# w_val decoded one tile per block, and two small matrix groups per block formed in the layer-1 banks

## The chip, the cores and the metric

One core of a Trainium2 chip runs the whole program. The metric is the device time of one execution in microseconds (us), as the median of three runs. TensorE (PE in the profile, its weight loads PEld) multiplies and writes to PSUM, of which this kernel uses all eight banks; VectorE (DVE) and ScalarE (ACT) read PSUM and work on SBUF; GpSimd (POOL) works on SBUF alone; SyncE (SP) issues nearly all transfers.

## What is computed

Eight batches (blocks b = 0 to 7) of 512 tokens go through an attention against 32 state rows per head, a normalised feed-forward layer with ReLU, and a gated layer, all in float32. The reference, cut:

```python
a = softmax(scale * x @ state.T);  xread = a @ state            # 512 tokens a block
a2 = softmax(scale * state @ x.T); sread = a2 @ x               # 32 tokens a block
x = concat(xread, sread)                                        # (8, 544, 512)
xn = (x - mu) / sqrt(var + 1e-6) * g_ln
x = x + maximum(xn @ w_ch1, 0) @ w_ch2
gate = sigmoid(causal_conv5(x, conv_w)); val = x @ w_val
out = (gate * val) @ w_out
```

(The concatenation stands for the kernel's two parts: 8 blocks of 512 tokens and, as a ninth block, the 8 x 32 tokens of sread.) The weights arrive as 64-bit floats and are decoded on the chip.

## The kernel before

**Precision.** Every large product is made of three fp32r matmuls (`mm3`, L76 to L79: high times low, low times high, high times high), so the lines L77, L78 and L79 carry nearly all of TensorE's time. An operand is split into a high and a low half by `split_sb` (L72: an ACT copy at L73, a subtraction at L74 on DVE or POOL).

**Loop.** `segment` (L590) goes through a block in 16 steps f, one for each 128 rows of the hidden layer. TensorE's order is written out by hand (the calls stand under `manual_schedule` for PE); the other engines' orders are made by a scheduler that goes by `at_prio` values and by its own estimate of when inputs are ready. In a step, TensorE computes layer 1 of step f (six matmuls of 512 columns into one of the two `ps_mm` banks, called h), then layer 2 of step f-1 (`second`, twelve matmuls into the four `ps_acc` banks). Layer 1's result goes through ACT (`hid`, L646) and DVE (L648) and is layer 2's operand in the next step.

**Matrix groups.** Layer 1 does not multiply the normalised tokens with `w_ch1`: for every quarter q of the hidden layer, `m_steps(b, q)` (L131) first multiplies the block's states into `w_ch1`. A group is eight small matmuls (L137, 64 rows by 32 columns of the array each, 512 columns of data, float32), four into the bank mp[0] and four into mp[1]; DVE then reads each bank once (L143, into `mb`) and ACT (L73) and POOL (L74, DVE in blocks 0 and 1) split it into `m`. There are 32 groups, four for each block, made at f = 1, 5 and 9 for the block's next quarter and at f = 13 for the next block's first. The banks come from the pool `ps_at` of two, which the scores (L188), the transposes (L261) and the column sums (L298) use too. Before, a group stands ahead of layer 1 of its step.

**Background.** At the end of each step `next(bg)` advances a generator. In blocks 2 to 7 it is `background(b)` (L910): first `x1_var` (L339), the variance of the block, whose last part (`rstd_of`, L301) comes after four empty steps; then `attention_steps(b + 1)` (L405) for the next block: scores (L188, same shape as the matrix groups, into two `ps_at` banks), the two softmaxes on DVE and ACT (L192 to L223, L242 to L253), the transposes (L261, full array) and `sread` (L275, small matmuls); then the next loads. After the last step of block 2 comes `prep_weights` for `w_val` (L902): four tiles, each loaded (L470, 512 KB) and decoded by `decode_split` (ACT L485 and L487, DVE L493, L495, L496, L500, then the split: ACT L73, DVE L74) into a tile called `raw`. At a block's last step whatever is left of the generator is run out.

**Block boundary.** Layer 2 of step 15 is drained by DVE (L675, four reads of the `ps_acc` banks, each followed by an addition L678); in step 1 of the next block `x1_group` (L313) writes the four `ps_acc` banks (L318), and ACT (L325) and DVE (L323) read two each.

## Time and profile before

| what | value |
|---|---|
| median of three runs | 910.47 us (910.41 to 911.41) |
| profiled execution: its own time | 910.09 us |
| its span, first to last instruction | 908.0 us |
| PE busy | 887.1 us (98% of the span) |
| DVE, ACT, POOL busy | 595.7, 381.9, 216.3 us |
| mean granted TensorE clock | 0.996 |

The profiled execution lies 0.38 us under the median. Sums below are made against its time. The granted clock is full (1.00) in every block. A full-size matmul (128 x 512) is shown 0.39 us long, but they are pipelined: starts lie 0.23 us apart. So gaps on TensorE are read from the starts, and "PE busy" says little; where TensorE stood still is seen in the lengths of equal stretches and in the idle times of the timeline.

### The profile page before, as it was taken

How to read it: one execution, taken by the hardware profiler on the slowest of the kernel's cores; microseconds unless marked ns; L12 is line 12 of the kernel's file. 1: busy time of each engine (PE TensorE's matmuls, PEld its weight loads, DVE VectorE, ACT ScalarE, POOL GpSimd, SP SyncE). 2: the span in 40 equal slices, each digit the busy share in tenths (PEclk: the TensorE clock that was granted, in tenths of full speed). 3: DMA queues.
4: the chain of work that ended last, by engine and by line, in shares of the span. 5: the costliest groups of instructions: out<-in, count | busy, mean ns of one | idle time of the engine just before them, and what ended most of it. 6: DMA issues, size and time to landing. Idle time of an engine off the chain costs nothing.

```text
span 908.0 us, 12667 instructions
## 1 busy us (share of the span) xinstructions
PE 887.1 (98%) x4987; PEld 668.5 (74%) x4988; DVE 595.7 (66%) x1030; ACT 381.9 (42%) x699; POOL 216.3 (24%) x172
## 2 busy tenths in 40 slices
PE   8988989999999999999999999999999999999998
PEld 3345657777777677777777777777789988888886
DVE  6998998486366663445437246342469799988870
ACT  4755654144253433324234233332327555455532
POOL 0001020012322522522342152253200023432100
PEclk9999999999999999999999999999999999999999
DMA  9932220022013111110111110110121212222122
GB/s 363 375 116 76 73 74 1 1 96 99 8 43 96 73 50 51 49 49 2 51 50 47 50 47 1 27 47 1 47 93 48 93 50 90 93 94 93 54 86 70
DMA packets 26667, 66.44 MB, mean 73 GB/s; under 512 B 10864, under 2 KB 13040, under 8 KB 22512
## 3 DMA queue, kind: packets, MB, share of 16 engines
q1 hardware_dynamic: 25984, 65.24, 20.1%
q8 instruction: 39, 0.64, 0.3%
q10 hardware_dynamic: 624, 0.40, 0.2%
q14 instruction: 20, 0.16, 0.1%
HBM read 47.80 MB, written 17.83 MB: 72 GB/s over the span
## 4 chain that ended last, share of the span: by engine, by line
PE 81%; DVE 12%; DMA 3%; ACT 1%; issue 1%; SPq 0%; DVEq 0%; ACTq 0%
PE acc L77 15%; PE acc L79 15%; PE acc L78 15%; PE mm L77 9%; PE mm L78 8%; PE mm L79 8%; PE at L137 3%; PE at L77 2%; PE at L79 2%; PE at L78 2%; DVE w L496 1%; DVE w L500 1%; DMA x1d<-t 1%; DVE hid L648 1%; DVE raw L496 1%
## 5 line engine op out<-in xcount | busy, mean ns | idle before, releaser
L77 PE MATMUL acc<-hid,w 128*128 128x512 f32 (+1 forms) x560 | 213.0, 380 | 2.2 <-DVE x L323 1.3
L78 PE MATMUL acc<-hid,w 128*128 128x512 f32 (+1 forms) x560 | 211.7, 378 | 0.0
L79 PE MATMUL acc<-hid,w 128*128 128x512 f32 (+1 forms) x560 | 211.6, 378 | 0.0
L648 DVE SCALAR_TENSOR_TENSOR hid<-mm,hid 128x512 fp32r<-128x512 f32 (+1 forms) x140 | 92.0, 657 | 141.4 <-ACT hid L646 141.2
L646 ACT ACTIVATE hid<-mm 128x512 fp32r<-128x512 f32 (+2 forms) x144 | 82.4, 572 | 216.6 <-PE mm L79 212.9
L77 PEld LDWEIGHTS acc<-hid,w 128*128 128x128 f32 x560 | 105.4, 188 | 25.3 <-DVE hid L648 2.2
L77 PE MATMUL mm<-ahl,m 128*128 128x512 f32 (+1 forms) x312 | 120.3, 385 | 0.0
L79 PEld LDWEIGHTS acc<-hid,w 128*128 128x128 f32 x560 | 105.4, 188 | 19.9
L78 PEld LDWEIGHTS acc<-hid,w 128*128 128x128 f32 x560 | 105.5, 188 | 19.5
L78 PE MATMUL mm<-ahl,m 128*128 128x512 f32 (+1 forms) x312 | 115.5, 370 | 0.3 <-DVE m L74 0.3
L79 PE MATMUL mm<-ahl,m 128*128 128x512 f32 (+1 forms) x312 | 115.5, 370 | 0.0
L724 DVE SCALAR_TENSOR_TENSOR ahl<-big,cw,ahl 128x508 f32<-128x508 f32 (+3 forms) x128 | 101.8, 845 | 0.2
L74 POOL TENSOR_TENSOR m<-mb,m 128x512 fp32r<-128x512 f32 x48 | 65.4, 1377 | 142.3 <-ACT m L73 142.3
L77 PEld LDWEIGHTS mm<-ahl,m 128*128 128x128 f32 x312 | 59.1, 189 | 40.7 <-issue 28.3
L73 ACT ACTIVATE m<-mb 128x512 fp32r<-128x512 f32 x62 | 39.0, 629 | 81.6 <-DVE mb L143 81.2
L79 PEld LDWEIGHTS mm<-ahl,m 128*128 128x128 f32 x312 | 59.0, 189 | 10.1
L78 PEld LDWEIGHTS mm<-ahl,m 128*128 128x128 f32 x312 | 59.2, 190 | 9.2 <-DVE m L74 1.0
L710 POOL TENSOR_TENSOR w<-big,w 128x512 fp32r<-128x512 f32 x24 | 38.6, 1636 | 93.1 <-ACT w L708 93.1
L143 DVE SCALAR_TENSOR_TENSOR mb<-cs,sbn,at 128x512 f32<-128x512 f32 x62 | 43.5, 743 | 21.9 <-PE at L137 20.9
L79 PE MATMUL acc<-w,raw 128*128 128x512 f32 (+1 forms) x144 | 54.4, 378 | 0.0
L78 PE MATMUL acc<-w,raw 128*128 128x512 f32 (+1 forms) x144 | 54.4, 378 | 0.0
L77 PE MATMUL acc<-w,raw 128*128 128x512 f32 (+1 forms) x144 | 54.4, 378 | 0.0
(178 smaller groups left out, 1332.1 us busy)
## 6 DMA issues: line engine op xcount, KB each, us to landing
w<-in_w SPq DMA_DIRECT2D x20, 512.0 KB, 7.1
big<-in_xT SPq DMA_DIRECT2D x8, 1024.0 KB, 4.9
big<-in_xk SPq DMA_DIRECT2D x8, 1024.0 KB, 5.6
x2d<-x SPq DMA_DIRECT2D x8, 1024.0 KB, 3.9
big<-x2d SPq DMA_DIRECT2D x8, 1024.0 KB, 4.8
out<-hid SPq DMA_DIRECT2D x16, 512.0 KB, 2.8
raw<-in_w SPq DMA_DIRECT2D x12, 512.0 KB, 6.7
raw<-in_wval SPq DMA_DIRECT2D x4, 512.0 KB, 3.6
```

Source lines behind the costliest of these rows:

```text
L73: nc.scalar.activation(hi, src, AF.Copy)
L74: eng.tensor_tensor(lo, src, hi.bitcast(F32), op=ALU.subtract)
L77: nc.tensor.matmul(acc, lhsT=wh, rhs=xl, start=first, stop=False)
L78: nc.tensor.matmul(acc, lhsT=wl, rhs=xh, start=False, stop=False)
L79: nc.tensor.matmul(acc, lhsT=wh, rhs=xh, start=False, stop=last)
L137: nc.tensor.matmul(mp[u][32 * p:32 * p + 32, :], lhsT=stg[r, p, :], rhs=w1s[4 * q + p][r], start=True, stop=True)
L143: a = nc.vector.scalar_tensor_tensor(mb, cs[:, q], sbn[:, u], mp[u], op0=ALU.mult, op1=ALU.add)
L496: a = nc.vector.tensor_scalar(h[:, :, 0, 1], h[:, :, 1, 1], 0x8000, 0x4000, op0=ALU.bitwise_and, op1=ALU.bitwise_or)
L646: marks["act"] = nc.scalar.activation(hid[:, 0], h, AF.Relu)
L648: marks["dve"] = nc.vector.scalar_tensor_tensor(hid[:, 1], h, 0.0, hid[:, 0].bitcast(F32), op0=ALU.max, op1=ALU.subtract)
L710: nc.gpsimd.tensor_tensor(lo, src, hi.bitcast(F32), op=ALU.subtract)
L724: t = nc.vector.scalar_tensor_tensor(g[:, j:], x[:, :n - j], cw_sb[:, k, PAD - j:TAPS - j], g[:, j:], op0=ALU.mult, op1=ALU.add)
```

## The change

1. `m_steps` takes a flag `mm`: with it, the two banks come from `ps_mm`, the pool of layer 1's h. In every group the order of the eight matmuls becomes four for mp[0], then four for mp[1], where they alternated.
2. In blocks 2 to 6, the groups of f = 5 and f = 9 use that flag and are formed after layer 2 of the step, directly ahead of the background's work, with another priority for their readers (`base - 500` where `base - 1500` stood).
3. `x1_var` has one empty step less and `attention_steps` one more behind the first softmax: variance, scores, softmaxes and transposes come one step earlier, `sread` and the loads stay. In block 7 an empty step keeps the sread block where it was.
4. `w_val` is no longer decoded at the end of block 2: in step 3 of blocks 3, 4, 5 and 6 one tile is loaded and decoded.

```diff
-    def m_steps(b, q):
+    def m_steps(b, q, mm=False):
         stg, _, sbn, _ = coef[b]
-        mp = [at_ps([P, S]) for _ in range(2)]
-        for p in range(KT):
-            for u in range(2):
+        mp = [ps(ps_mm, "mm", [P, S]) if mm else at_ps([P, S]) for _ in range(2)]
+        for u in range(2):
+            for p in range(KT):
                 r = slice(64 * u, 64 * u + 64)
...
         hl = halves_of(sqs[0], S)
-        yield
         yield
         yield
         yield
...
         softmax1_out(b)
         mean_terms(b)
         yield
+        yield
         sread(b)
...
+            later = 1 < b < B - 1 and f in (5, 9)
-            if b < B and unit is not None and f % QF == (2 if unit == (1, 0) else 1) and not fresh:
+            if b < B and unit is not None and f % QF == (2 if unit == (1, 0) else 1) and not fresh and not later:
                 at_prio(base - 1500)
                 m_steps(*unit)
...
             pend[0] = second
+            if later:
+                at_prio(base - 500)
+                m_steps(*unit, mm=True)
             at_prio(base + 500)
             next(bg, None)
...
+    val_weights = []
+
     def background(b):
         yield
-        yield from x1_var(b)
+        if b == 3:
+            val_weights.append(prep_weights(wval, wv, ["raw"] * KT))
+        for i, _ in enumerate(x1_var(b)):
+            if i == 2 and val_weights:
+                next(val_weights[0], None)
+            yield
         if b + 1 < B:
             yield from attention_steps(b + 1)
         else:
+            yield
             yield from sread_block_steps()
-        if b == 2:
-            yield from prep_weights(wval, wv, ["raw"] * KT)
```

How the built programs' instructions stand, at three places. In the rows, an operation's output is left of the arrow and its operands right, with the buffers' numbers; lines of the changed kernel behind L600 are one to four higher than those of the kernel before.

Place A, TensorE in block 4, before, at step 5: the end of layer 2 of step 3, the group for q = 2 (in `at` banks), layer 1 of step 5.

```order
L79 MATMUL acc3_589_3275<-hid_599_3327,w2_3_92_443 128x512
L137 MATMUL at_602_3364<-w1_4_156_772,stg_509_2811 32x512
L137 MATMUL at_603_3365<-w1_4_156_772,stg_509_2811 32x512
L137 MATMUL at_602_3364<-w1_4_156_772,stg_509_2811 32x512
L137 MATMUL at_603_3365<-w1_4_156_772,stg_509_2811 32x512
L137 MATMUL at_602_3364<-w1_5_167_830,stg_509_2811 32x512
L137 MATMUL at_603_3365<-w1_5_167_830,stg_509_2811 32x512
L137 MATMUL at_602_3364<-w1_5_167_830,stg_509_2811 32x512
L137 MATMUL at_603_3365<-w1_5_167_830,stg_509_2811 32x512
L77 MATMUL mm_607_3383<-ahl_543_3010,m_575_3224 128x512
```

The same group now, behind layer 2 of step 4, and directly behind it the scores of the next block (six more L188 rows follow, then layer 1 of step 6, whose bank is that of `mm_601`).

```order
L79 MATMUL acc3_580_3239<-hid_595_3325,w2_4_112_516 128x512
L137 MATMUL mm_601_3370<-w1_4_156_772,stg_498_2753 32x512 x2
L137 MATMUL mm_601_3370<-w1_5_167_830,stg_498_2753 32x512 x2
L137 MATMUL mm_602_3371<-w1_4_156_772,stg_498_2753 32x512 x2
L137 MATMUL mm_602_3371<-w1_5_167_830,stg_498_2753 32x512 x2
L188 MATMUL at_609_3397<-big_551_3092,st_raw_549_3088 32x512
L188 MATMUL at_610_3398<-big_551_3092,st_raw_549_3088 32x512
```

The group moved behind eighteen full matmuls and stands in a row with the scores, which in the kernel before come a step later, alone. At step 9 the group likewise stands directly ahead of the eight transposes L261.

Place B, DVE at the end of block 2 and the beginning of block 3, before: the third and fourth tile of `w_val` (`c_455`, `c_458`) between the reads of the `ps_acc` banks (L675), the matrix group (L143) and the copies L323.

```order
L495 TENSOR_SCALAR c_455_2515<-c_455_2515 128x512
L496 TENSOR_SCALAR raw_454_2513<-raw_454_2513 128x512
L675 TENSOR_TENSOR t2_465_2573<-acc1_365_1971,t2_463_2562 128x512
L648 SCALAR_TENSOR_TENSOR hid_462_2559<-mm_461_2552,hid_462_2559 128x512
L675 TENSOR_TENSOR t2_466_2579<-acc2_366_1975,t2_463_2562 128x512
L500 ISA c_455_2515<-raw_454_2513,c_455_2515 128x1024
L675 TENSOR_TENSOR t2_467_2585<-acc3_367_1979,t2_463_2562 128x512
L143 SCALAR_TENSOR_TENSOR mb_471_2601<-cs_7_84,sbn_393_2141,at_468_2590 128x512
L143 SCALAR_TENSOR_TENSOR mb_472_2605<-cs_7_84,sbn_393_2141,at_469_2591 128x512
L74 TENSOR_TENSOR raw_456_2522<-c_455_2515,raw_456_2522 128x512
L323 COPY x1_473_2609<-acc1_475_2611 128x512
L493 TENSOR_SCALAR c_458_2527<-c_458_2527 128x512
```

The same place now (L676 and L649 are L675 and L648 of before).

```order
L649 SCALAR_TENSOR_TENSOR hid_450_2511<-mm_449_2504,hid_450_2511 128x512
L676 TENSOR_TENSOR t2_453_2525<-acc1_365_1971,t2_451_2514 128x512
L676 TENSOR_TENSOR t2_454_2531<-acc2_366_1975,t2_451_2514 128x512
L676 TENSOR_TENSOR t2_455_2537<-acc3_367_1979,t2_451_2514 128x512
L143 SCALAR_TENSOR_TENSOR mb_459_2553<-cs_7_84,sbn_391_2119,at_456_2542 128x512
L143 SCALAR_TENSOR_TENSOR mb_460_2557<-cs_7_84,sbn_391_2119,at_457_2543 128x512
L323 COPY x1_461_2561<-acc1_463_2563 128x512
L323 COPY x1_461_2561<-acc3_465_2565 128x512
```

The decode rows are gone from the boundary; what is left there is the sequence that the boundary of blocks 3 and 4 has in the kernel before.

Place C, DVE in block 4, steps 3 to 6, before: layer 1's results of steps 3 and 4, the group for q = 2, the result of step 5.

```order
L648 SCALAR_TENSOR_TENSOR hid_599_3327<-mm_598_3320,hid_599_3327 128x512
L648 SCALAR_TENSOR_TENSOR hid_601_3349<-mm_600_3342,hid_601_3349 128x512
L143 SCALAR_TENSOR_TENSOR mb_605_3375<-cs_7_84,sbn_510_2813,at_602_3364 128x512
L143 SCALAR_TENSOR_TENSOR mb_606_3379<-cs_7_84,sbn_510_2813,at_603_3365 128x512
L648 SCALAR_TENSOR_TENSOR hid_608_3390<-mm_607_3383,hid_608_3390 128x512
```

Now: the five operations of one `w_val` tile between the results of steps 3 and 4, the variance's two (L304, L306), and the group's two reads behind the result of step 5, ahead of the scores' transposes L192.

```order
L649 SCALAR_TENSOR_TENSOR hid_590_3291<-mm_589_3284,hid_590_3291 128x512
L493 TENSOR_SCALAR c_592_3308<-c_592_3308 128x512
L496 TENSOR_SCALAR raw_591_3306<-raw_591_3306 128x512
L495 TENSOR_SCALAR c_592_3308<-c_592_3308 128x512
L500 ISA c_592_3308<-raw_591_3306,c_592_3308 128x1024
L74 TENSOR_TENSOR raw_593_3315<-c_592_3308,raw_593_3315 128x512
L649 SCALAR_TENSOR_TENSOR hid_595_3325<-mm_594_3318,hid_595_3325 128x512
L304 STREAM_TRANSPOSE t2_597_3343<-at_596_3340 128x512
L306 TENSOR_SCALAR rstd_598_3345<-t2_597_3343 128x16
L649 SCALAR_TENSOR_TENSOR hid_600_3355<-mm_599_3348,hid_600_3355 128x512
L143 SCALAR_TENSOR_TENSOR mb_604_3381<-cs_7_84,sbn_499_2755,mm_601_3370 128x512
L143 SCALAR_TENSOR_TENSOR mb_605_3385<-cs_7_84,sbn_499_2755,mm_602_3371 128x512
```

What moved: the tile's five operations came in, and the two L143 went from ahead of the result of step 5 to behind it. On DVE at step 9 the group's L143 likewise follow the result of step 9, ahead of which stand one L217 and two L223 of the first softmax.

## Rows read from the trace of the kernel before

**Rows 1.** The page's chain of work that ended last, shares by engine.

```profile
PE 81%; DVE 12%; DMA 3%; ACT 1%; issue 1%; SPq 0%; DVEq 0%; ACTq 0%
```

**Rows 2.** Blocks 2, 3, 4: length; PE, PEld, DVE, ACT, POOL busy; granted clock; DMA.

```profile
217.25:294.12 76.87, 76.75 (x468) 57.66 (x461) 45.65 (x80) 29.83 (x54) 23.30 (x18) 1.00 0.17 58
294.12:374.96 80.84, 78.86 (x468) 57.68 (x461) 43.99 (x76) 27.59 (x50) 28.24 (x22) 1.00 0.14 49
374.96:450.63 75.67, 75.67 (x469) 57.47 (x461) 36.71 (x66) 25.21 (x46) 26.22 (x22) 1.00 0.13 45
```

**Rows 3.** PE timeline, beginning of block 3: start, length, operation, idle before and releaser.

```profile
294.12 2.63 PE L318 MATMUL acc<-aT,sn_raw 32*64 32x512 f32 x12
297.99 0.50 PE L77 MATMUL mm<-ahl,m 128*128 128x512 f32 x1
...
301.79 0.39 PE L79 MATMUL acc<-hid,w 128*128 128x512 f32 x1
303.49 0.50 PE L77 MATMUL acc<-hid,w 128*128 128x512 f32 x1 [1.31 <-DVE x L323]
```

**Rows 4.** DVE timeline of the same place.

```profile
292.05 1.86 DVE L496 TENSOR_SCALAR raw<-raw 128x512 uint16<-128x512 uint16 x1
...
298.17 1.10 DVE L74 TENSOR_TENSOR raw<-c,raw 128x512 fp32r<-128x512 f32 x1
...
300.38 0.47 DVE L493 TENSOR_SCALAR c<-c 128x512 f32<-128x512 f32 x1 [0.51 <-ACT c L485]
300.88 1.40 DVE L495 TENSOR_SCALAR c<-c 128x512 uint32<-128x512 uint32 x1
...
302.73 0.71 DVE L323 COPY x<-acc 128x512 f32<-128x512 f32 x1
```

**Rows 5.** One group on the tiles `raw`, 270 to 306.5 us: least, median, greatest ns.

```profile
L500 DVE CUSTOM_DVE_ANT_0 c<-raw,c x4: 671/693/808, 282.1 to 303.4; 128x1024 uint16<-128x1024 uint16 x4
```

**Rows 6.** PE timeline in block 4 and at its beginning.

```profile
374.96 1.21 PE L318 MATMUL acc<-aT,sn_raw 32*64 32x512 f32 x16
376.10 0.50 PE L77 MATMUL mm<-ahl,m 128*128 128x512 f32 x1
...
392.81 0.39 PE L79 MATMUL acc<-hid,w 128*128 128x512 f32 x1
393.13 1.09 PE L137 MATMUL at<-w,stg 64*32 64x512 f32 x16
394.15 0.50 PE L77 MATMUL mm<-ahl,m 128*128 128x512 f32 x1
394.49 0.39 PE L78 MATMUL mm<-ahl,m 128*128 128x512 f32 x1
...
421.79 1.04 PE L261 MATMUL at<-ident,t 128*128 128x128 f32 x8
422.58 0.48 PE L77 MATMUL mm<-ahl,m 128*128 128x512 f32 x1
...
430.93 1.10 PE L275 MATMUL mm<-big,t 128*32 128x64 f32 x64
431.96 1.09 PE L137 MATMUL at<-w,stg 64*32 64x512 f32 x16
432.98 0.50 PE L77 MATMUL mm<-ahl,m 128*128 128x512 f32 x1
```

**Rows 7.** DVE timeline in block 4.

```profile
391.15 0.69 DVE L648 SCALAR_TENSOR_TENSOR hid<-mm,hid 128x512 fp32r<-128x512 f32 x1 [3.33 <-ACT hid L646]
394.39 1.41 DVE L143 SCALAR_TENSOR_TENSOR mb<-cs,sbn,at 128x512 f32<-128x512 f32 x2 [2.55 <-PE at L137]
```

**Rows 8.** Groups by line and shape over the whole span: the softmax's operations.

```profile
L223 DVE TENSOR_TENSOR ahl<-aT,ahl 128x512 fp32r<-128x512 f32 x16 | 16.0, 1008 | 0.1
L217 DVE STREAM_TRANSPOSE aT<-t 128x512 f32<-128x512 f32 x16 | 10.8, 686 | 0.0
```

**Rows 9.** What PE waited for over the span, us in total, times, longest.

```profile
PE at L77 <- DVE mb L143: 0.9, 1, 0.9
```

**Rows 10.** PE timeline in block 0/1: four column tiles that share all rows.

```profile
125.82 1.07 PE L155 MATMUL at<-w,g 128*32 128x512 f32 x8
```

## The prediction

> **What bounds the kernel now.** I read the chain of work that ended last first: 81% of the span lies on TensorE [rows 1], so a change is worth what TensorE's starts gain. The busy share (98%) cannot say where it loses, because overlapping matmuls count as busy. So I cut the span at the same point of each block, the first L318, and compared lengths [rows 2]. Block 4 takes 75.67 us (blocks 5 and 6 the same within 0.01), block 2 takes 76.87, block 3 takes 80.84, at the same full granted clock and with the same number of matmuls within one. Blocks 3 and 4 run the same program, apart from `w_val`'s decode, of which the last two tiles reach into the boundary before block 3. The excess of block 3 is 80.84 - 75.67 = 5.17 us.
>
> The timelines say where. In block 3 the L318 group holds TensorE from 294.12 to 297.99, 3.87 us [rows 3]; in block 4 from 374.96 to 376.10, 1.14 us [rows 6]. That is 2.73 us. Then L77 at 303.49 comes 1.70 us after the start before it, where 0.23 is the rule, with DVE's copy L323 named as releaser [rows 3]: 1.47 us more. The rest of about 1 us is small change behind it. DVE's own rows show why L323 was late [rows 4]: it stands in the queue behind a decode that waited 0.51 us for ACT, and whose operations were stretched while GpSimd worked on the block's additions (L496 1.86 us, L495 1.40, L74 1.10).
>
> **The change part by part.** *Decode out of the boundary.* DVE's order at the beginning of block 3 becomes the one that block 4 has now, with no decode row in it. Block 3 should then take block 4's time: -5.17 us. Block 2 keeps its own 1.20 us (76.87 - 75.67), since there DVE itself does the four additions L678 and nothing of that is touched.
>
> *Decode in blocks 3 to 6.* Nothing gets lighter; five DVE operations and three ACT operations per tile now stand between the layer-1 results of steps 3 and 4. Before the latter DVE idles 3.33 us today [rows 7]. With every operation at the longest that its rows show (0.47 + 1.40 + 1.86 + 0.81 + 1.10) [rows 4, 5] the tile takes 5.64 us, which makes the result of step 4 late by 2.3 us. That result ends at 391.15 + 0.69 = 391.84 today, and layer 2 asks for it some 3.1 us later (393.13 without the group, two column-sum matmuls and six of layer 1, eight starts of 0.23, gives 394.95) [rows 6, 7]. So 2.3 is covered by 3.1 and I cost it at nothing; without the cover it would be up to 2.3 for each of four tiles. The four loads stand on SP's queue behind a state load and ahead of the next block's x; a tile is wanted about two steps later, and I cost them at nothing too.
>
> *Two groups per block beside other small matmuls (5 blocks).* A lone group costs TensorE 1.22 us: 393.13 comes 0.32 after the start before it (0.09 over the rule), the group lasts 1.02 to 394.15, and the next start is 0.34 away (0.11 over) [rows 6]. Where two kinds of small matmuls stand in a row, as L275 and L137, the second follows after 1.03 and takes its 1.02, and the 0.20 of one pair of crossings is paid once [rows 6]. So at step 5, beside the scores of the same shape, 0.20 is saved. But layer 1 of the next step now takes the bank of mp[0]. It is free when the group has ended (1.09 after its start, 394.22), DVE has begun L143 (394.39, 0.17 later, a short wait instruction included), read the bank (1.41 for two, so about 0.75 for the first) and released it (302.73 + 0.71 = 303.44, and TensorE starts at 303.49, 0.05) [rows 3, 4, 6, 7]: 2.06 us after the group's start. The scores cover 1.02 + 1.02 = 2.04, so the wait at step 5 is 0.02. It also caps the saving: if the scores slipped into the group's tail, which no row shows, TensorE would wait for the bank instead. At step 9 the cover is the group's 1.02 and the transposes' 0.79 (421.79 to 422.58) [rows 6]: 1.81, so TensorE waits 0.25. The transposes use the whole array as layer 1 does, so both crossings of the group stay; I take a saving of 0.05 between 0 and 0.10. Per block: -0.20 + 0.02 + 0.25 - 0.05 = +0.02, over five blocks +0.1 us, between -1.1 (L143 begins at once, without the 0.17: no wait at step 5, 0.08 at step 9, where the full 0.10 is saved) and +1.2 (nothing saved at step 9, and every wait 0.2 longer at one of the two places).
>
> *Four matmuls for mp[0], then four for mp[1] (all 32 groups).* The eight lie on eight different parts of the array and start together, so a group should keep its 1.02 us. Where mp[1]'s bank is not yet free, as in blocks 0 and 1, the first four run sooner and L143 of mp[0] with them, but the group's end is that of its last four, as before. DVE's order changes in blocks 0 and 1 follow from it; one wait of 0.9 us for L143 [rows 9] may go. DVE is the fuller engine there, and its work is the same, so most of such a gain returns as a later wait. I take -0.2, between -1.2 and +1.0 (one such wait gone, or one more).
>
> *Order of the variance and the softmaxes.* One step earlier, same instructions, on PE, DVE, ACT and POOL alike. The matrix parts m of the two moved groups now have about two steps (8 us) instead of three before layer 1 wants them, and on GpSimd their L74 stand behind the variance's operation. The reads take 1.41 [rows 7] and the splits follow them in pairs; I cost it at nothing, and if they were late TensorE would wait at steps 8 and 12.
>
> The sum against the profiled execution: 910.09 - 5.17 + 0.1 - 0.2 = 904.8 us. The median of three lies 0.38 above that execution, so the forecast is **905.2 us** for the median.
>
> **The rivals.** *A, the groups in layer 1's banks wait for DVE (slower).* Place: step 9 of blocks 2 to 6. On DVE, the result of step 9 and then L143 stand behind one L217 and two L223, 0.69 + 2 x 1.01 = 2.70 us [rows 8]. If these are not done when the group ends, layer 1 of step 10 waits for all of it: 5 x 2.70 = 13.5 us, 918.7 us. It decides when the five places lose over (5.27 + 1.82)/5 = 1.4 us each, where 5.27 is the gain above and 1.82 is 0.2%. Against it: those 2.70 us begin behind the result of step 8, a whole step (18 starts of 0.23, 4.1 us) ahead of the result of step 9, and between layer 1 of step 9 and the group lies layer 2 (12 starts, 2.7 us), in which ACT and DVE (0.69 [rows 7]) can finish that result. Chance 4%.
>
> *B, four matmuls on the same rows do not overlap (slower).* If four matmuls on the same rows hold each other up, the four of mp[1] begin only when those of mp[0] are done, and a group takes at least twice its 1.02 us: 32 x 1.02 = 32.6 us, 937.8 us; slower from (5.27 + 1.82)/32 = 0.22 us per group on. Against it: L155 puts four matmuls (two records each) on the same 128 rows and different columns, and all eight records end within 1.07 us [rows 10]. The Trainium skill (TensorE: Matmul & The Clock Gate, The mechanism in Part 3) says that weight loads overlap running matmuls only where the row group differs; by it the new order would be this rival, and the trace does not bear it out at L155. Chance 1%.
>
> *C, part of it is given back.* Each of the ten places loses 0.3 us more than I allow, because ACT and DVE have the splits, a transposed copy and the mean terms to do between the group and the next layer-1 result, and that result comes late: 905.2 + 10 x 0.3 = 908.2 us. Chance 11%.
>
> *D, the boundary's loss is not the decode's.* If block 3 keeps it, because the four GpSimd additions and the copies alone delay L323, only the small terms are left: 910.47 + 0.1 - 0.2 = 910.4 us. Against it: block 4 has these same additions and copies, and loses nothing. Chance 4%.
>
> *E, more than the sum.* L143 begins at once and the early waits go: 910.47 - 5.17 - 1.1 - 1.2 = 903.0 us or less. Chance 4%.
>
> **How the numbers follow.** The forecast has 76%. Its own bounds are E's 903.0 and 910.47 - 5.17 + 1.2 + 1.0 = 907.5; C begins inside that and is centred at 908.2. The range from 902.9 to 907.9 leaves out A, B, D, half of E and most of C, together under 2 in 10. A measurement of this kernel can tell about 0.2%, 1.8 us, so "faster" is under 908.65 and "slower" over 912.3. Faster: the forecast, E and most of C, 88%. Same: D and the end of C, 7%. Slower: A and B, 5%.
>
> **What the profile would show.** Right: block 3 from L318 to L318 within 0.5 us of block 4; L318 at its beginning at 1.14 us and no PE wait on L323; the decode operations of one tile in step 3 or 4 of blocks 3 to 6 and no PE gap there; L188 about 1.02 us behind L137 at step 5; a PE wait on DVE L143 of about 0.2 us at step 10 and near zero at step 6; groups of 1.02 us throughout. Wrong: PE waits of over 0.5 us on L143 in blocks 2 to 6 (A or C), groups longer than 1.1 us (B), block 3 still at 80 us (D), or a stall after step 4 on `hid`, which would say that the decode's cover was too thin.

## The result, and the profile after

| what | before | after |
|---|---|---|
| median | 910.94 us (four runs, 910.41 to 911.51) | 903.61 us (four runs, 903.50 to 904.07) |
| profiled execution, its own time | 910.09 us | 903.50 us |
| its span | 908.0 us | 901.7 us |

The ratio is 0.9919, with a 95% interval from 0.9906 to 0.9931: faster by 7.3 us, 0.8%. (The median of before was 910.47 over the first three runs; a fourth one at 911.51 moved it.) The forecast was 905.2, range 902.9 to 907.9. The profiled executions differ by 6.6 us, their spans by 6.3, and it is these 6.3 us that can be followed from row to row.

The chain of work that ended last (shares of the span by engine, after) lies still more on TensorE than in [rows 1]:

```profile
PE 84%; DVE 12%; issue 1%; ACT 1%; DMA 1%; SPq 0%; ACTq 0%; DVEq 0%
```

The span cut at the first L318 of each block, as in [rows 2] (after; stretch, length, then busy time and instructions of PE, PEld, DVE, ACT and POOL, granted TensorE clock, DMA share, GB/s). The first row is blocks 0 and 1, the others blocks 2 to 4. (In blocks 0 and 1 the mean granted clock was 0.98 before too, not the 1.00 that the text on the profile before gives for every block; it was 0.50 there for 6.8 us before and for 10.2 us after, so the clock did not make these blocks shorter.)

```profile
0.00:216.22 216.22, 202.55 (x1126) 125.92 (x1126) 175.82 (x349) 109.03 (x199) 15.80 (x18) 0.98 0.35 129
216.22:293.20 76.98, 76.83 (x468) 57.77 (x460) 40.10 (x70) 25.19 (x46) 22.94 (x19) 1.00 0.13 44
293.20:368.61 75.41, 75.41 (x468) 57.66 (x461) 39.73 (x71) 26.83 (x49) 25.64 (x22) 1.00 0.15 52
368.61:444.05 75.44, 75.44 (x468) 57.65 (x461) 39.74 (x71) 26.84 (x49) 25.64 (x22) 1.00 0.15 52
```

Against before that is -1.03 us in blocks 0 and 1 (217.25 there), +0.11 in block 2, -5.43 in block 3 and -0.23 in block 4 (blocks 5 and 6: -0.22 each). Block 7 and what follows take 0.75 us more (306.77 against 306.02). The sum is -6.3: the whole difference of the spans. (The rest of the 7.3: outside its span the profiled execution of after is 0.3 us shorter too, and the median of before lies 0.85 above its profiled execution, that of after 0.1.)

**The beginning of block 3 (-5.43).** TensorE's timeline there (after; start, duration, engine, line, operation, out<-in, count), where [rows 3] showed L318 at 3.87 us and a wait for L323 at the tenth start of layer 2, its fourth bank:

```profile
293.20 1.20 PE L318 MATMUL acc<-aT,sn_raw 32*64 32x512 f32 x16
294.34 0.50 PE L77 MATMUL mm<-ahl,m 128*128 128x512 f32 x1
...
298.15 0.39 PE L79 MATMUL acc<-hid,w 128*128 128x512 f32 x1
298.38 0.39 PE L77 MATMUL acc<-hid,w 128*128 128x512 f32 x1
```

L318 to L77 takes 1.14 us, and layer 2 goes on to its fourth bank at 298.38, 0.23 after the start before, without a wait. Why L318 took 2.73 us more in the kernel before is seen in two rows of DVE and one of TensorE (before), which [rows 3] and [rows 4] leave out:

```profile
295.53 0.81 DVE L500 CUSTOM_DVE_ANT_0 c<-raw,c 128x1024 uint16<-128x1024 uint16 x1
296.26 0.68 DVE L675 TENSOR_TENSOR t<-acc,t 128x512 f32<-128x512 f32 x1
296.99 1.07 PE L318 MATMUL acc<-aT,sn_raw 32*64 32x512 f32 x4 [0.24 <-DVE t L675]
```

The last four L318 write a bank that DVE had to read first, and that read, L675, stood behind decode operations in DVE's queue. So the decode held TensorE in two ways: between the reads L675 (2.73 us) and ahead of the copy L323 (1.47). Now DVE's timeline there has no decode left in it (compare [rows 4]); the copies L323 stand right behind L143:

```profile
291.40 1.88 DVE L676 TENSOR_TENSOR t<-acc,t 128x512 f32<-128x512 f32 x3
293.31 1.41 DVE L143 SCALAR_TENSOR_TENSOR mb<-cs,sbn,at 128x512 f32<-128x512 f32 x2
294.64 1.28 DVE L323 COPY x<-acc 128x512 f32<-128x512 f32 x2
```

**The decode in its new place (0).** DVE's timeline between the layer-1 results L649 of two steps of block 3 (in brackets the idle time before, and what ended it):

```profile
305.39 0.69 DVE L649 SCALAR_TENSOR_TENSOR hid<-mm,hid 128x512 fp32r<-128x512 f32 x1 [3.39 <-ACT hid L647]
306.00 0.42 DVE L493 TENSOR_SCALAR c<-c 128x512 f32<-128x512 f32 x1
306.51 0.76 DVE L496 TENSOR_SCALAR raw<-raw 128x512 uint16<-128x512 uint16 x1
307.05 0.46 DVE L495 TENSOR_SCALAR c<-c 128x512 uint32<-128x512 uint32 x1
307.55 0.69 DVE L500 CUSTOM_DVE_ANT_0 c<-raw,c 128x1024 uint16<-128x1024 uint16 x1
308.94 0.69 DVE L74 TENSOR_TENSOR raw<-c,raw 128x512 fp32r<-128x512 f32 x1 [0.70 <-ACT raw L73]
309.55 0.68 DVE L649 SCALAR_TENSOR_TENSOR hid<-mm,hid 128x512 fp32r<-128x512 f32 x1
```

A tile takes 306.00 to 309.63, 3.6 us, 0.70 of it waiting for ACT. GpSimd is not at work on large tiles here, so L496 takes 0.76 where it took 1.86 at the boundary. The list of PE's waits names none between 216.22 and 594.94; small ones are seen only in the distances between starts, below.

**The two groups (-0.22 per block).** TensorE at step 5 of block 4, and DVE's L143 that reads the group:

```profile
391.04 0.39 PE L79 MATMUL acc<-hid,w 128*128 128x512 f32 x1
391.36 1.09 PE L137 MATMUL mm<-w,stg 64*32 64x512 f32 x16
392.24 1.06 PE L188 MATMUL at<-big,st_raw 64*32 64x512 f32 x16
393.29 0.50 PE L77 MATMUL mm<-ahl,m 128*128 128x512 f32 x1
393.63 0.39 PE L78 MATMUL mm<-ahl,m 128*128 128x512 f32 x1
```

```profile
392.49 1.41 DVE L143 SCALAR_TENSOR_TENSOR mb<-cs,sbn,mm 128x512 f32<-128x512 f32 x2 [2.36 <-PE mm L137]
```

From L79 to L78, 2.59 us pass. Two lone sets cost 1.22 each on top of the ordinary starts; here both together cost 2.59 - 2 x 0.23 = 2.13, so 0.32 is saved. The scores begin 0.88 us behind the group, not 1.02: they start inside its tail. L77 follows 1.05 behind the scores instead of 1.02, since it takes the bank of mp[0], which DVE reads from 392.49 on: that bank is back 1.93 us after the group's start. Step 9 of the same block, with the transposes:

```profile
409.54 0.39 PE L79 MATMUL acc<-hid,w 128*128 128x512 f32 x1
409.85 1.09 PE L137 MATMUL mm<-w,stg 64*32 64x512 f32 x16
410.87 1.09 PE L261 MATMUL at<-ident,t 128*128 128x128 f32 x8
411.87 0.50 PE L77 MATMUL mm<-ahl,m 128*128 128x512 f32 x1
412.20 0.40 PE L78 MATMUL mm<-ahl,m 128*128 128x512 f32 x1
```

L79 to L78 is 2.66 us, less two starts 2.21. Before, the lone group cost 1.22, and the transposes 0.88 (0.23 + 0.79 from the start before them to L77 [rows 6], and L78 0.31 later, less two starts). So step 9 loses 0.10. L77 stands 0.99 behind the first transpose instead of 0.79: there is the wait for mp[0]'s bank, though the list of waits does not name it, because the transposes before it still count as running.

**Block 7 (+0.85) was not foreseen.** TensorE and its weight loads at the end of step 4 of block 7:

```profile
613.03 0.62 PE L298 MATMUL at<-t,ones 128*128 128x512 f32 x2
613.58 1.94 PE L137 MATMUL at<-w,stg 64*32 64x512 f32 x16
615.45 0.50 PE L77 MATMUL mm<-ahl,m 128*128 128x512 f32 x1
```

```profile
614.46 0.15 PEld L137 LDWEIGHTS at<-w,stg 64*32 64x32 f32 x8 [0.72 <-DVE t L304]
```

This group still takes the two attention banks. The earlier variance put its column total L298, which takes one of them, directly ahead. The four matmuls for mp[1] wait until DVE's transpose L304 has read it, and the group holds TensorE for 1.87 us instead of 1.02. Before, L298 stood 5.2 us behind the group. (In the stretch from block 7 on it shows as 0.75: the length of that stretch varies, from 305.5 to 306.0 us over the five kernels whose variance in block 7 is the old one: before, experiments 1, 2, 5 and 11.)

**Blocks 0 and 1 (-1.03), block 2 (+0.33 less the 0.22 of its groups).** PE's waits from 48.5 to 160 us (engine, waited for, us in total, times, longest): of before, besides [rows 9], one that is gone:

```profile
PE at L275 <- DVE t L304: 1.1, 1, 1.1
```

After, TensorE waits 0.28 us for ACT at the same L275 and 0.36 for an L74 at 55.9, and a wait for L244 grew from 3.11 to 3.35; two waits of 0.3 us are gone as well. Ahead of 48.5 a wait for L143 takes 1.2 us and took 0.5.

At the beginning of block 2, DVE and TensorE's weight loads (after):

```profile
217.42 0.74 DVE L143 SCALAR_TENSOR_TENSOR mb<-cs,sbn,at 128x512 f32<-128x512 f32 x1
218.08 0.68 DVE L679 TENSOR_TENSOR x<-t,x 128x512 f32<-128x512 f32 x1
218.68 0.74 DVE L143 SCALAR_TENSOR_TENSOR mb<-cs,sbn,at 128x512 f32<-128x512 f32 x1
219.34 1.41 DVE L679 TENSOR_TENSOR x<-t,x 128x512 f32<-128x512 f32 x1
220.67 1.28 DVE L323 COPY x<-acc 128x512 f32<-128x512 f32 x2
```

```profile
221.40 0.19 PEld L77 LDWEIGHTS acc<-hid,w 128*128 128x128 f32 x1 [0.46 <-DVE x L323]
```

With four matmuls for mp[0] first, the scheduler puts the first L143 ahead of one more addition L679; the split L74 of what it made begins on GpSimd at 218.90, and the last addition takes 1.41 us beside it instead of 0.68. (In the kernel before the last addition had begun 0.17 us ahead of that L74; there, and again in experiment 10, the addition kept its 0.68, and the L74 took 1.67 us instead of 1.29.) L323 is late, and TensorE waits 0.19 us more than an ordinary start, and 0.11 at the start after it. The Trainium skill (GPSIMD Engine Reference, 1. Specifications) says that GpSimd contends with DVE instructions that have two SBUF inputs; L679 has two, and its 1.41 us beside L74 agrees.

### The profile page after: what moved, and what is told of

Same layout as the page of the kernel before. It is cut to its first block, busy times and chain, and to the rows that moved or that the text cites. A ratio compares the mean times of both kernels' runs of the same rounds, so it can differ in the third digit from the quotient of the medians.

```text
span 901.7 us, 12630 instructions
## 1 busy us (share of the span) xinstructions
PE 884.0 (98%) x4988; PEld 669.7 (74%) x4988; DVE 593.1 (66%) x1030; ACT 382.2 (42%) x699; POOL 211.9 (24%) x172
## 4 chain that ended last, share of the span: by engine, by line
PE 84%; DVE 12%; issue 1%; ACT 1%; DMA 1%; SPq 0%; ACTq 0%; DVEq 0%
PE acc L77 16%; PE acc L79 16%; PE acc L78 16%; PE mm L77 9%; PE mm L78 8%; PE mm L79 8%; PE at L137 2%; PE at L79 2%; PE at L77 2%; PE at L78 2%; DVE w L500 1%; PE mm L137 1%; DVE w L496 1%; DVE raw L496 1%; DVE w L493 1%
## 5 line engine op out<-in xcount | busy, mean ns | idle before, releaser
L77 PE MATMUL acc<-hid,w 128*128 128x512 f32 (+1 forms) x560 | 212.9, 380 | 0.4 <-DVE hid L649 0.4
L78 PE MATMUL acc<-hid,w 128*128 128x512 f32 (+1 forms) x560 | 211.6, 378 | 0.0
L79 PE MATMUL acc<-hid,w 128*128 128x512 f32 (+1 forms) x560 | 211.6, 378 | 0.0
L649 DVE SCALAR_TENSOR_TENSOR hid<-mm,hid 128x512 fp32r<-128x512 f32 (+1 forms) x140 | 91.8, 656 | 153.3 <-ACT hid L647 153.2
L77 PEld LDWEIGHTS acc<-hid,w 128*128 128x128 f32 x560 | 105.6, 189 | 23.1 <-DVE hid L649 1.0
L79 PEld LDWEIGHTS acc<-hid,w 128*128 128x128 f32 x560 | 105.5, 188 | 19.9
L78 PEld LDWEIGHTS acc<-hid,w 128*128 128x128 f32 x560 | 105.7, 189 | 19.6
L77 PE MATMUL mm<-ahl,m 128*128 128x512 f32 (+1 forms) x312 | 119.3, 382 | 0.0
L78 PE MATMUL mm<-ahl,m 128*128 128x512 f32 (+1 forms) x312 | 115.7, 371 | 0.4 <-DVE m L74 0.4
L79 PE MATMUL mm<-ahl,m 128*128 128x512 f32 (+1 forms) x312 | 115.4, 370 | 0.0
L74 POOL TENSOR_TENSOR m<-mb,m 128x512 fp32r<-128x512 f32 x48 | 62.1, 1314 | 122.3 <-ACT m L73 122.3
L73 ACT ACTIVATE m<-mb 128x512 fp32r<-128x512 f32 x62 | 38.9, 632 | 110.6 <-DVE mb L143 110.3
L77 PEld LDWEIGHTS mm<-ahl,m 128*128 128x128 f32 x312 | 59.0, 189 | 33.7 <-issue 15.7
L79 PEld LDWEIGHTS mm<-ahl,m 128*128 128x128 f32 x312 | 59.1, 189 | 10.1
L78 PEld LDWEIGHTS mm<-ahl,m 128*128 128x128 f32 x312 | 59.2, 190 | 10.0 <-DVE m L74 1.5
L78 PE MATMUL acc<-w,raw 128*128 128x512 f32 (+1 forms) x144 | 54.3, 377 | 0.0
L79 PE MATMUL acc<-w,raw 128*128 128x512 f32 (+1 forms) x144 | 54.3, 377 | 0.0
L77 PE MATMUL acc<-w,raw 128*128 128x512 f32 (+1 forms) x144 | 54.3, 377 | 0.0
L676 DVE TENSOR_TENSOR t<-acc,t 128x512 f32<-128x512 f32 (+1 forms) x44 | 28.0, 659 | 27.9 <-PE acc L79 27.9
```

The source lines that it names most:

```text
L73: nc.scalar.activation(hi, src, AF.Copy)
L74: eng.tensor_tensor(lo, src, hi.bitcast(F32), op=ALU.subtract)
L77: nc.tensor.matmul(acc, lhsT=wh, rhs=xl, start=first, stop=False)
L78: nc.tensor.matmul(acc, lhsT=wl, rhs=xh, start=False, stop=False)
L79: nc.tensor.matmul(acc, lhsT=wh, rhs=xh, start=False, stop=last)
L649: marks["dve"] = nc.vector.scalar_tensor_tensor(hid[:, 1], h, 0.0, hid[:, 0].bitcast(F32), op0=ALU.max, op1=ALU.subtract)
```

## The experiments

Times are medians; blocks are cut at L318 as above. Where the profile is not shown, a kernel's block lengths were read from the same view. Part 3 of the change in blocks 2 to 6 and the readers' other priority were not run alone.

**1. The decode alone.** The kernel before with part 4 of the change alone: the edits of `background` and `val_weights`, without the empty step ahead of the sread block.

> The kernel before with the decode of w_val alone moved (one tile per block in blocks 3 to 6, at the third step of the variance's schedule); the groups, their order and the steps of variance and softmaxes stay as before. Theory (the boundary's loss is the decode's): block 3 from L318 to L318 falls from 80.84 to 75.7 us, blocks 4 to 6 stay at 75.67, nothing else moves; 5.2 us less than the kernel before, about 905.7 us. Rival 1 (the step shift is needed for it, because otherwise the decode lies in the way of the variance): blocks 3 to 6 at 76.5 to 78 us, 908 us or more. Rival 2 (the GpSimd additions alone delay L323): block 3 stays above 79 us, 910 us.

Measured: 904.53 us against 910.34, ratio 0.9942 (0.9930 to 0.9953). Blocks 3 and 4 of its profile:

```profile
294.23:369.90 75.67, 75.67 (x469) 57.44 (x461) 39.36 (x71) 26.89 (x49) 26.26 (x22) 1.00 0.15 52
369.90:445.56 75.66, 75.66 (x468) 57.41 (x460) 39.37 (x71) 26.89 (x49) 26.27 (x22) 1.00 0.15 52
```

Block 3 lost exactly its excess of 5.17 us, and the four tiles cost nothing where they are now (blocks 3 to 6 at 75.66 to 75.67). Both rivals fall. The median gained 0.6 us more than the 5.2 expected; the spans of the profiles differ by 5.4, of which 0.3 lies in block 7 and what follows.

**2. The order in the groups alone.** The kernel before, with the loops over `u` and `p` in `m_steps` exchanged.

> The kernel before with the order inside the matrix groups alone changed (four matmuls for mp[0], then four for mp[1]). Theory (DVE reads mp[0] earlier; good where PE waits for L143 in blocks 0 and 1, bad at the start of block 2, where the earlier L143 now stands ahead of the additions L678): blocks 0 and 1 shorter by 0.6 to 1.0 us, block 2 longer by 0.3, blocks 3 to 6 unchanged, 910.2 to 910.7 us. Rival (the 1.0 us by which the changed kernel is ahead at the start of block 2 is only where its trace begins and how its first loads landed): blocks 0 and 1 unchanged, 911.2 us with the loss of block 2.

Measured: 909.71 against 910.34, ratio 0.9993 (0.9983 to 1.0002). The profile has -1.20 in blocks 0 and 1, more than the theory's 0.6 to 1.0, +0.32 in block 2, as the theory said, and +0.80 in block 3, which it did not say:

```profile
293.24:374.88 81.64, 80.02 (x469) 58.93 (x461) 44.28 (x76) 27.64 (x50) 27.71 (x22) 0.98 0.14 48
```

DVE's timeline there shows why: in the new order of DVE all four decode operations of the last tile stand ahead of the second L323, where L500 stood behind it before.

```profile
302.88 0.69 DVE L500 CUSTOM_DVE_ANT_0 c<-raw,c 128x1024 uint16<-128x1024 uint16 x1
303.49 0.68 DVE L323 COPY x<-acc 128x512 f32<-128x512 f32 x1
```

That copy begins 10.25 us after L318, against 8.61 before. So the order of the groups and the place of the decode are not independent.

**3. All but the decode.** The changed kernel with `background` as it was before (four tiles at the end of block 2).

> The changed kernel with the decode of w_val left where it was before (all four tiles at the end of block 2). Theory (the parts add up): the 5.43 us that block 3 gained come back and the rest of the gain, 1.9 us, stays: 909.0 us, block 3 at 80.6, blocks 4 to 6 at 75.44. Rival (with mp[0] read earlier DVE's queue at the boundary is shorter, and the decode there costs less): block 3 at 78 to 79.5 us, 906.5 to 908 us.

Measured: 909.19 against 910.34, ratio 0.9990 (0.9982 to 0.9999). Block 3 takes 81.61 us: the decode's place is worth 6.2 us (81.61 - 75.41) with the new order in the groups, and 5.17 with the old one. The rival wanted a smaller loss at the boundary; it is larger. Not all of the 6.2 need be DVE's: in this profile TensorE ran at a granted clock of 0.50 from 296 to 302 and came to layer 2's fourth bank at 304.26, 0.58 us after L323 had ended. Block 5 takes 75.78, because at its step 9 L143 began 0.57 us behind the first transpose and not 0.19, with DVE idle before it; why is not known.

**4. All but the order in the groups.** The changed kernel with the two loops in the old order.

> The changed kernel with the old order inside the groups (mp[0] and mp[1] in turn). Theory (the order matters only to when DVE reads mp[0]; the 0.14 us by which the scores start inside the tail of the group at step 5 comes from the equal form of the two sets of matmuls): L188 still 0.88 us behind L137 at step 5, blocks 4 to 6 at 75.44; blocks 0 and 1 lose 0.6 to 1.0, block 2 gets its 0.33 back; 904.0 us. Rival (it is the new order that lets the scores start early, because the parts of mp[0] come free first): L188 1.02 us behind L137, blocks 2 to 6 longer by 0.14 each, 904.7 us.

Measured: 904.52 against 910.34, ratio 0.9936 (0.9924 to 0.9948). L188 still stands 0.88 us behind L137, so the early start comes with the two sets and not with the order; the rival falls. L77 stands 1.10 behind L188 instead of 1.05, and at step 9 1.04 behind L261 instead of 0.99: blocks 3 to 6 take 75.50 instead of 75.41 to 75.45. Blocks 0 and 1 take 216.96, 0.74 more than the changed kernel; block 2 takes 76.70, 0.28 less.

**5. Block 7 as it was.** The changed kernel, but:

```diff
-        yield
-        yield
+        for _ in range(3 if b == B - 1 else 2):
+            yield
         rstd_of(b, hl, S)
```

(and without the empty step that the change put ahead of the sread block).

> The changed kernel, but in block 7 alone the variance stays where it was before the change (one step later). Theory (block 7 of the changed kernel loses 0.85 us inside its group at step 4: the column total L298 has just taken one of the two attention banks, and the four matmuls for mp[1] wait until DVE's transpose L304 has read it): the group lasts 1.02 instead of 1.87 us, 0.8 us less than the changed kernel, 902.8 us. Rival (the loss is GpSimd's: its L74 come later in block 7 because they stand behind L437 and L308): the group at 1.87 gets shorter, but layer 1 waits for m instead, 903.6 us.

Measured: 902.27 against 910.86, ratio 0.9911 (0.9896 to 0.9926). The group of block 7 lasts 1.02 us and the list shows no wait for m in its place; the last L298 of that block is reached 0.83 us earlier. The loss was the bank's.

**6. The groups without cover.** The changed kernel, the two groups in layer 1's banks but at f = 4 and 8.

> The changed kernel with the two groups of blocks 2 to 6 formed one step earlier, still in layer 1's banks, but no longer next to the scores and the transposes (steps 4 and 8 instead of 5 and 9). Theory (what makes layer 1's banks harmless is the cover: the bank of mp[0] comes back 2.01 us after the group's start): at step 8 the next L77 starts about 2.0 us after the group's start instead of 1.02, at step 4, with the two L298 as a cover, about 2.0 too; the scores and the transposes pay their own entry and exit again. Per block 0.85 + 0.89 us more, five blocks 8.7, 912.3 us. Rival (L143 has the bank free by the group's end, no cover needed): only the 0.22 per block that the changed kernel gained are lost, 904.7 us.

Measured: 911.68 against 910.86, ratio 1.0009 (1.0000 to 1.0018). Blocks 3 to 6 take 77.11 to 77.16, 1.7 more than after. Step 8 of block 4:

```profile
409.80 1.09 PE L137 MATMUL mm<-w,stg 64*32 64x512 f32 x16
411.81 0.50 PE L77 MATMUL mm<-ahl,m 128*128 128x512 f32 x1 [0.92 <-DVE mb L143]
```

2.01 us from the group's start to L77, the number that the prediction built from four rows as 2.06. At step 4 it is 2.01 as well (1.02 to L298, 0.99 more to L77). This is the wait if too little covers it.

**7. The groups in the attention banks.** The changed kernel with `m_steps(*unit)` where it has `mm=True`.

> The changed kernel with the two groups at the same places, but in the two attention banks (as before the change), which the scores and the transposes behind them also take. Theory (the scores then wait for DVE to read both banks: 1.2 + 0.75 + 0.66 us after the group's start): L188 about 2.7 us behind L137 instead of 0.88 at step 5, the last transpose some 1.15 us later at step 9; (1.8 + 1.15) x 5 = 14.7 us more, 918 us. Rival (the bank does not matter, as at the other places where a group in these banks stands next to a set of small matmuls): 903.6 us.

Measured: 917.09 against 910.86, ratio 1.0069 (1.0052 to 1.0086). Blocks 3 to 6 take 78.1, 2.7 more than after. PE's waits in blocks 2 to 6:

```profile
PE at L261 <- DVE mb L143: 4.6, 5, 0.9
PE at L188 <- DVE mb L143: 4.2, 5, 0.8
```

In block 4 the first L188 begins 1.93 us behind L137 and the others, which need the second bank too, 2.59, near the 2.7 expected. So the new place without the other pool costs 13 us more than the changed kernel (14.7 were expected).

**8. One tile per block, in two other places.** The changed kernel with `next(val_weights[0], None)` at the end of `background` of blocks 2 to 5 (step 15), and, in a second kernel, at the very beginning of `background` of blocks 3 to 6, where DVE's order has the tile between the last L676 and L323.

> The changed kernel with the decode of w_val still one tile per block, but at the end of blocks 2 to 5: a tile's DVE work stands between the results of steps 14 and 15, ahead of the four L676. Theory (what hurt before is decode work between L676 and the copies L323, and two tiles at once; a single tile of 3.6 us fits between two layer-1 results, where DVE idles 3.4 us in each step): blocks 3 to 6 within 0.3 us of 75.44, at most 905 us. Rival (any tile next to the boundary costs at least a quarter of the 5.17 us): 1.3 us in each of four blocks, 908.8 us or more.

> The changed kernel with the decode one tile per block, but in blocks 3 to 6 right at the beginning: on DVE a tile stands between the last L676 and the copies L323. Theory (the place makes the loss: L323 waits for a tile's DVE work, 3.6 us undisturbed to 5.6 us beside GpSimd's additions, less some 0.6 of slack; TensorE waits for L323): blocks 3 to 6 longer by 3 to 5 us each, 916 to 923 us. Rival (it was the two tiles in a row; one fits in): under 1 us per block, 907 us or less.

Measured: at step 15, 903.38 against 910.16, ratio 0.9933 (0.9915 to 0.9951), blocks 3 to 6 at 75.43 to 75.46, as worked out. Before the copies, 915.49, ratio 1.0057 (1.0044 to 1.0070), blocks 3 to 6 at 78.35 to 78.42, 2.9 us more each, a little under the 3 to 5 that were expected. DVE at the beginning of block 3 of the second kernel, and PE's waits in its blocks 3 to 6:

```profile
295.09 1.82 DVE L496 TENSOR_SCALAR raw<-raw 128x512 uint16<-128x512 uint16 x1
```

```profile
PE acc L77 <- DVE x L323: 5.0, 8, 1.1
PE acc L77 <- ACT x L325: 1.9, 4, 0.5
```

L318 keeps its 1.14 us here, since the tile stands behind the last L676. TensorE waits for the copies, and not for DVE's alone: ACT's first L325 stands behind an L73 that waits for an L143 which the tile has delayed. So a loss does not need several tiles in a row: one tile between the last L676 and the copies, stretched where GpSimd's additions run, costs 2.9 us. The larger part of what block 3 lost before, 2.73 us from decode between the reads themselves, does not occur in this kernel. Ahead of the four L676 the same tile is free.

**9. Step 5 alone.** The changed kernel with `later` for f == 5 only; the group of step 9 is again formed alone at the beginning of its step, in the attention banks.

> The changed kernel with the group of step 9 back in the attention banks at the beginning of that step, alone; the group of step 5 stays next to the scores. Theory (per block step 5 gained 0.32 us and step 9 lost 0.10): blocks 2 to 6 shorter by 0.10 each, 75.34 us, 903.1 us in all. Rival (alone, the group of step 9 is as late as next to the transposes, or its two banks are not read in time for the transposes): blocks 2 to 6 at 75.44 or more, 903.6 us or more.

Measured: 902.87 against 910.86, ratio 0.9915 (0.9900 to 0.9929). Blocks 3 to 6 take 75.31 to 75.35: 0.10 less each, as worked out. The group of step 9 was better off before.

**10. The old order in one group.** The changed kernel with the eight matmuls of the group (2, 1), at the beginning of block 2, in turn:

```diff
-        for u in range(2):
-            for p in range(KT):
+        for i in range(2 * KT):
+            for p, u in [(i // 2, i % 2) if (b, q) == (2, 1) else (i % KT, i // KT)]:
```

> The changed kernel with the old order inside one group alone, the one at the beginning of block 2. Theory (at the boundary of block 2 DVE itself does the additions L679; with mp[0] ready first, L143 goes ahead of one of them, GpSimd's L74 starts 0.6 us earlier and stretches the last L679 to 1.41 us, and TensorE waits for L323): block 2 shorter by 0.33, 903.3 us. Rival (the wait for L323 comes from elsewhere): 903.6 us, block 2 at 76.98.

Measured: 902.94 against 910.16, ratio 0.9927 (0.9911 to 0.9944). Block 2 takes 76.65, 0.33 less; the last L679 takes 0.69 us again. (In this profile blocks 0 and 1 took 218.07 us, after a beginning at a lower granted clock.)

**11. The three together.** The edits of 5, 9 and 10.

> The changed kernel with three pieces put back: the variance of block 7 one step later, the group of step 9 alone in the attention banks at the beginning of its step, the old order in the one group at the beginning of block 2. Theory (the three losses are independent): 903.61 - 0.82 - 0.50 - 0.33 = 902.0 us. Rival (they share a cover, so part of one comes back in the next block): 902.6 to 903.2 us.

Measured: **901.37 us** against 910.16, ratio 0.9902 (0.9889 to 0.9915), the shortest of all. Blocks 2 and 3:

```profile
216.07:292.62 76.55, 76.42 (x469) 57.83 (x461) 39.05 (x70) 25.63 (x46) 22.81 (x19) 1.00 0.12 44
292.62:367.95 75.33, 75.33 (x468) 57.63 (x460) 39.46 (x71) 27.17 (x49) 25.18 (x22) 1.00 0.15 52
```

Block 2 is 0.43 shorter than after (0.33 + 0.10), blocks 3 to 6 about 0.10 each, and block 7 with what follows 1.26 (0.85 expected; that stretch varies by 0.5 us between kernels with the same block 7). Its interval overlaps that of the changed kernel (0.9906 to 0.9931); what sets it apart are the three places, each of which shows its gain in the trace.

## Why the prediction was right, point by point

| term | forecast | measured |
|---|---|---|
| decode out of the boundary | -5.17 | -5.17 with the old order in the groups (experiment 1), -6.2 with the new one (3) |
| decode in blocks 3 to 6 | 0 | 0 (1) |
| two groups per block, five blocks | +0.1 | -1.1: five times -0.32 at step 5 and +0.10 at step 9 |
| order in all groups | -0.2 | -0.7: -1.0 in blocks 0 and 1, +0.33 in block 2 |
| variance and softmaxes one step earlier | 0 | +0.85 in block 7 (5); nothing is left over for it in blocks 3 to 6 |
| sum | -5.3 | -6.1 of the 6.3 us by which the spans differ |

**The boundary: right, in place and size.** Block 3 was to become like block 4 and did so within 0.03 us. The reading that two equal blocks differ by what is done differently in them carried the forecast. It rested on one view and one comparison, not on any count of busy time. The mechanism was given for the wait for L323 only, 1.47 us of the 5.17; that L318's 2.73 us came from decode operations ahead of the reads L675 was not said, and the comparison of lengths did not need it.

**The decode's cover: right.** The bound of 5.64 us for a tile was made from durations stretched beside GpSimd; the tile took 3.6. DVE idled 3.4 us there, and no layer-1 result was late enough for TensorE.

**Step 5: right mechanism, two sizes off.** The saving less the wait was put at 0.20 - 0.02 and came out at 0.32. The scores began in the group's tail, 0.88 us behind its start and not 1.02, and the bank of mp[0] was back after 1.93 us and not 2.06, because L143 began 1.13 us after the group's start and not 1.26. Both were needed: the prediction named the early start as one that no row shows and that the bank's release would cap, and with 2.06 it would have been capped at a saving of under 0.2. Where the first size went wrong can be seen: the pair L275 and L137 [rows 6], from which 1.03 was taken, has two different shapes, while the group and the scores are of one form (16 records each, 64 by 32).

**Step 9: right mechanism and sign.** Forecast +0.25 - 0.05 = +0.20, measured +0.10: a wait of about 0.20 and a saving of 0.10, the upper end of what was allowed. That this half of the change is a small loss was forecast, and experiment 9 confirms it. The bank came back after 2.01 us here (1.02 + 0.99).

**The order in the groups: mis-sized, and one effect missed.** It was costed at -0.2 between -1.2 and +1.0. The wait of [rows 9] did go, and so did one of 1.1 us for L304; but only about half of their 2.0 us came back in other waits, where most was expected to. The 1.0 us in blocks 0 and 1 is typical rather than exact: over the eleven kernels with the new order these blocks took 215.4 to 218.1 us, with 216.1 in the middle, and 216.96 to 217.34 over the three with the old one; two of the eleven lie above all three. Missed was block 2: the text said that nothing of its boundary is touched, but the order on DVE is made by readiness, and mp[0] was ready earlier.

**The variance: this step failed.** It was costed at 0 as "same instructions, on PE, DVE, ACT and POOL alike". The instructions are the same, but in block 7 the moved column total met a group for which nothing had changed, and both want the same two banks. Moving a step means asking at each place that it now passes which banks are held there, in the blocks that are treated as exceptions too.

**The rivals.** A (a queue on DVE) did not come up: at step 9 L143 began 0.19 us after the first transpose. B fell: in blocks 2 to 6 every group takes 1.02 us to the next start, or 0.88 to the scores. D fell with experiment 1. C (0.3 us more at each of the ten places) did not come up: five places were better than forecast by 0.14 us, five by 0.10. E's premises came true in part: the early waits went and L143 began sooner than allowed for. The sign that was set for B, a group longer than 1.1 us, did show, in block 7 alone and from another cause, a bank.

**What was luck.** Two terms came out 1.2 and 0.5 us better than forecast and a third 0.85 worse. That the sum was off by only 0.8 is in part this cancelling. The median came out 1.6 below the forecast; the other 0.8 are 0.2 that were followed to no place, 0.3 outside the span and 0.3 by which the median lies closer to the profiled execution than before.

## What to carry to other kernels

If blocks run the same program, cut the span at the same instruction of each and compare the lengths: the excess of one of them is the price of what is done in it alone. Moving that work to a place where the engine that TensorE waits for idles brought the whole of it here. Side work ahead of an operation without slack made TensorE wait (2.9 us for a tile ahead of the copies), and in another step it cost nothing. A bank that is borrowed from another use is as cheap as what covers its release (1.93 to 2.01 us here), so check cover and holder at every place that an edit moves, including the first and last block.

## What had not been expected of the hardware

**Two sets of small matmuls of one form follow each other without a pause.** Group and scores stand 0.88 us apart where a group followed by layer 1 or by the transposes takes 1.02, in each of the five blocks and with either order inside the group. The records lie in four passes of eight, which start 0.45, 0.43 and 0.43 us apart at step 5 of block 4. Being small is not enough: at the block boundaries L318 (32 rows by 64 columns, 16 records) follows a group after 1.02 us. Whether equal shape or the equal number of rows is what allows it was not tried.

**TensorE's clock fell inside a boundary.** In experiment 2, TensorE hung on DVE between 293.24 and 297.68 (L318 took 4.44 us until the next L77, against 3.87 before), and the granted clock was 0.50, the level of 1.2 GHz, from 298 to 301; by 302 it was 1.00 again. In the kernel before, the same stall, 0.6 us shorter, left the clock at 1.00 throughout. In experiment 3 it fell at the same place and stayed low for longer. There the fall began between 295 and 296, less far into the stall (L318 had begun at 292.96) than the 3.87 us that left the clock untouched in the kernel before. So the length of the stall alone does not decide it. From the timelines of experiments 2 (first row) and 3:

```profile
300.00:301.00 1.00, 1.00 (x3) 0.77 (x3) 0.83 (x1) 1.00 (x3) 1.00 (x3) 0.50 0.88 369
```

```profile
296.00:302.00 6.00, 5.60 (x13) 3.21 (x14) 5.38 (x8) 3.92 (x7) 5.42 (x5) 0.50 0.75 272
```

In experiment 2 the slow stretch cost next to nothing, because TensorE waited for L323 behind it until 304.23. In experiment 3 no such wait was left.
